# Attention and gated MLP on one core: weight conversions given written places, loads placed further ahead, and a memory turn done by transpositions

## The chip, the cores and the metric

The kernel runs on one core of one Trainium2 chip. The time is device microseconds (us) of one execution; times of a kernel are the median of several runs. The core has a matrix engine (TensorE, here PE), a vector engine (VectorE, DVE), a scalar engine (ScalarE, ACT), a GpSimd engine (POOL) and a sync engine (SP) whose instruction queue issues nearly all DMA transfers. Each engine works through its own instructions in order and waits for the others through semaphores.

## The reference

Two stages. A causal attention over 4 batches, 8 heads, 576 positions and 64 dimensions is mixed with a recall from a memory matrix, and the result goes through a gated MLP of 2304 tokens (512 to 1536 to 512).

```python
local = softmax(scale * q @ k.T, causal) @ v
q_p   = where(q > 0, q, exp(q) - 1) + 1
mem   = (q_p @ M_prev) / (q_p @ z_prev + 1e-6)
g     = sigmoid(beta)
x     = g * mem + (1 - g) * local          # then [B*S, H*D] = 2304 x 512
out   = (silu(x @ w_gate) * (x @ w_val)) @ w_out
```

All inputs arrive wide: the weights are read as pairs of 32-bit words and converted on the chip into a high and a low part that TensorE takes one after the other.

## The kernel before

**Attention.** The 32 heads are done as 16 pairs (`Pair`). One turn of the loop over `n` computes the scores and exponentials of pair `n` and finishes pair `n-1` (`old`): it turns its weighted probabilities by transpositions on PE (`turned1`, `turned`; the records tr<-ident,ps, tr<-ident,pl and tr<-ident,p), recalls from the memory (`recall`; tr<-mm,ph), turns the recalled 128x128 blocks (`recalled`; tr<-ident,mem) into two PSUM banks called `first` and `rest`, and adds the probabilities times V on top of them (`values`; tr<-g,vp). ACT and DVE then read `first` and `rest` out (`leave`; xh, xl). Turned blocks are copied out of PSUM as `g` by ACT or DVE. PSUM has four banks for scores (`psS`, records s) and four for everything else (`psT`, records tr), given out in rotation by `rot`; a bank is written again only when its last reader is through.

**Order.** Instructions called through `pe`, `act`, `dve` and `pool` stay in the order of the program text. Instructions called through `ACT`, `DVE` and `SP` may be placed by a scheduler, which works from a simulated timeline; `later_by` lowers their priority. The engines then run the resulting order strictly.

**Weights.** The MLP's weights come as 36 "thirds" (12 blocks of the hidden dimension, three matrices each). For a third n, `raw_load(n)` transfers it (wraw, 512 KB), `raw_top(n)` makes `we` from it on ACT, and `third(n)` makes `wa` from both on DVE in three instructions (min/max, shift, or) and copies the high part on ACT (wgh, woh); `low_part` later makes the low part on DVE (wgl, wol). wdr and wdo are DRAM copies for later token blocks. Thirds 0 to 2 are converted during the attention, at loop turns 1 to 3 (`EARLY`), through the scheduler. Thirds 3 and 4 are loaded when the attention ends; the others follow, one per PE step, while the first token block of the MLP runs (`some`).

**MLP.** Three blocks of 768 tokens (`ORDER`), for each of which all 12 hidden blocks are gone through: `eight` in the first token block (steps of 12 matmuls s<-xp..,wg., alternating between two PSUM banks, `bank`), `seven` in the others, with the second product (woh, wol) in between. In `eight`, a step with gv=0 is read by ACT (Silu, zg and zh), one with gv=1 by DVE.

Of the kernel before, what the change touches and what calls it, by code (L numbers as in the profile page):

```python
# [9 lines left out]
F32 = mybir.dt.float32  # L10
F32R = mybir.dt.float32r
I32 = mybir.dt.int32
AF = mybir.ActivationFunctionType
ALU = mybir.AluOpType
# [12 lines left out]

P_LOAD = 400
ORDER = (0, 768, 1536)
EARLY = (1, 2, 3)  # L30
P_EARLY = 200
ACT_K = (0, 1)
ON_POOL = ("q", "k")
PS_S, PS_T = 4, 4
# [4 lines left out]
W_TOP = float.fromhex("0x1.dffffep+15")  # L39
# [4 lines left out]
def attention_moe(ctx: ExitStack, tc: tile.TileContext, qt, kt_, v, m, beta, wg, wv, wo, out):  # L44
    nc = tc.nc
    PE, ACT, DVE, POOL, SP = nc.tensor, nc.scalar, nc.vector, nc.gpsimd, nc.sync
# [3 lines left out]
    psT = ctx.enter_context(tc.tile_pool(name="psT", bufs=1, space=PSUM))  # L50
# [43 lines left out]
    def rot(pool, name, shape, dtype, n):  # L94
        held = slots.setdefault(name, [0, []])
        if len(held[1]) < n:
            held[1].append(pool.tile(shape, dtype, name=f"{name}{len(held[1])}"))
        held[0] += 1
        return held[1][(held[0] - 1) % n]
# [6 lines left out]
        return pool.tensor_scalar(dst, src, 1.0, 0.0, op0=ALU.mult, op1=ALU.add)  # L106

    def split_lo(dst, src, hi, kind=""):
        eng = pool if kind in ON_POOL else DVE
        return eng.tensor_tensor(dst, src, hi.bitcast(F32), op=ALU.subtract)  # L110

    ident = const.tile([128, 128], F32, name="ident")
# [42 lines left out]

    held, wout = {}, {}
    thirds = [(f, j) for f in range(NF) for j in range(3)]
    raws, tops, low_parts = {}, {}, []

    def raw_load(n, after=None):  # L160
        if n < len(thirds):
            f, j = thirds[n]
            raws[n] = rot(wp, "wraw", [128, 512, 2], I32, 2)
            ld = SP.dma_start(raws[n].rearrange("p a b -> p (a b)"), (wg, wv, wo)[j][f].bitcast(I32))
            if after is not None:
                follow(ld, after, "the loads that the attention waits for go first")

    def raw_top(act, n):
        if n < len(thirds):
            tops[n] = rot(wp, "we", [128, 512], F32, 2)  # L170
            act.activation(tops[n], raws[n][:, :, 1].bitcast(F32), AF.Prelu, scale=2.0**-111, alpha=2.0**32)

    def low_part(dve):
        while low_parts:
            f, j, a, oh, ol = low_parts.pop()
            dve.tensor_tensor(ol, a, oh.bitcast(F32), op=ALU.subtract)
            if j == 2:
                for i, o in enumerate((oh, ol)):
                    SP.dma_start(wdo[f, :, i], o.bitcast(F32))

    def third(act, dve, n):

        low_part(dve)
        if n >= len(thirds):
            return
        f, j = thirds[n]
        e, low = tops.pop(n), raws.pop(n)[:, :, 0]
        dve.tensor_scalar(e, e, W_TOP * 2.0**-111, -W_TOP * 2.0**-79, op0=ALU.min, op1=ALU.max)
        a = rot(wp, "wa", [128, 512], I32, 3)
        dve.tensor_scalar(a, e.bitcast(I32), 3, None, op0=ALU.logical_shift_left)  # L190
        dve.scalar_tensor_tensor(
            out=a, in0=low, scalar=29, in1=a, op0=ALU.logical_shift_right, op1=ALU.bitwise_or
        )
        if j == 0:
            held[f] = [rot(wp, f"wg{part}", [128, 1024], F32R, 2) for part in "hl"]
        if j == 2:
            wout[f] = oh, ol = [rot(wp, f"wo{part}", [128, 512], F32R, 3) for part in "hl"]
        else:
            c = slice(j * 512, j * 512 + 512)
            oh, ol = (x[:, c] for x in held[f])  # L200
            SP.dma_start(wdr[f, :, c], a.bitcast(F32))
        act.copy(oh, a.bitcast(F32))
        low_parts.append((f, j, a.bitcast(F32), oh, ol))

    with tc.tile_pool(name="sb", bufs=1, reuse_waits="tile") as sb:

# [17 lines left out]
        def pair_split(n, raw):  # L224
            qr, kr = raw
            q = [rot(sb, f"q{part}", [128, 640], F32R, NK) for part in "hl"]
            k = [rot(sb, f"k{part}", [128, 576], F32R, NK) for part in "hl"]
            early = n == 0
            (ACT.copy if n in ACT_K else split_hi)(k[0], kr)
            split_hi(q[0], qr[:, 128:768])  # L230

            def lows():
                split_lo(q[1], qr[:, 128:768], q[0], "" if early else "q")
                split_lo(k[1], kr, k[0], "" if early else "k")

            return q, k, lows

# [20 lines left out]
        class Pair:  # L258
# [128 lines left out]

            def recalled(self):

                rest, first = (rot(psT, "tr", [128, 512], F32, PS_T) for _ in range(2))  # L390
                self.av = first, rest
                y = self.mem.rearrange("p t j d -> p t (j d)")
                for t in (2, 3, 0, 1):
                    o = t % 2 * 128
                    pe.matmul(self.av[t // 2][:, o : o + 128], y[:, t], ident, start=(t % 2 == 0), stop=False, skip_group_check=True)

            def turned(self, t, h, *engs):

# [72 lines left out]
        pairs[0].load()  # L471
        gates()
        pairs[0].split()
        pairs[0].load_v()
        pairs[0].phi_parts()()
        pairs[1].load()
        pairs[0].lows()
        nothing = lambda *args: None
        ending = lambda: nothing
        for n in range(NP + 1):  # L480
            cur = pairs[n] if n < NP else None
            old = pairs[n - 1] if n > 0 else None
            after = pairs[n + 1] if n + 1 < NP else None
            exp = cur.exp if cur else nothing
            scores = cur.scores if cur else lambda t: nothing
            turned, turned1 = (old.turned, old.turned1) if old else (nothing, nothing)
            if cur:
                cur.begin()
            if old:
# [12 lines left out]
            turned1(1, act)  # L502
            exp(0, 1)
            exp(1, 0)
            turned(2, 0, dve)
            turned(2, 1, dve)
            exp(1, 1)
            scale = old.recall() if old else nothing
            if cur:
                cur.weighed(((0, 0), (0, 1), (1, 0), (1, 1)))  # L510
            scale()
            if after:
                after.lows()
            phi = after.phi_parts() if after else nothing
            reads = [scores(t) for t in range(2, 4)]
            reads[0](0)
            reads[0](1)
            exp(2, 0)
            exp(2, 1)
            turned(3, 0, act)  # L520
            turned(3, 1, dve)
            read4 = cur.scores4() if cur else nothing
            reads[1](0)
            turned(4, 0, act, dve)
# [12 lines left out]
            ending = old.leave() if old else lambda: nothing  # L537
            if n + 2 < NP:
                with later_by(P_LOAD):
                    pairs[n + 2].load()  # L540
            if after:
                after.load_v()
            if n in EARLY:
                with later_by(P_EARLY):
                    i = EARLY.index(n)
                    raw_load(i, loads[n + 1])
                    raw_top(ACT, i)
                    third(ACT, DVE, i)
                    low_part(DVE)

        ending()()

# [1 line left out]
    with tc.tile_pool(name="stg2", bufs=1, reuse_waits="tile") as stg2, \  # L554
# [209 lines left out]
        first = units[0][0]  # L764
        for p, i, j in (("p1", 0, 0), ("p2", 0, 1), ("p7", 1, 0), ("p4", 1, 1)):
            direct(first, p, i, j)
        raw_load(3)
        raw_load(4)
        before = None
        spreads = lambda mix, *what: [  # L770
            (high if kind == "h" else low)(mix, p, k) for kind, p in what for k in range(2)
# [2 lines left out]
        for n, unit in enumerate(units):  # L774
# [5 lines left out]
            again(n)  # L780
            if whole and left:
                def some(i):
                    if i == 3:
                        raw_top(act, 3)
                    third(act, dve, i)
                    raw_top(act, i + 1)
                    raw_load(i + 2)
                for k in range(3):
                    plan[k].append(lambda i=3 * n + 3 + k: some(i))
            if n < len(units) - 1 and units[n + 1][0] != first:  # L790
# [106 lines left out]
```

## Time and profile before

| | |
|---|---|
| median of 3 runs | 651.28 us (648.32 to 651.58) |
| the profiled execution | 653.73 us |
| its span, first to last instruction | 651.8 us |
| mean granted TensorE clock | 0.988 of full speed |
| attention, up to the first MLP matmul | 212.1 us |
| PE busy | 627.0 us, 96% of the span |
| DVE, ACT, POOL busy | 460.0, 362.7, 156.0 us |

The time of the profiled execution is 1.9 us longer than its span, which is what lies before the first and behind the last instruction. A PE record's duration is modelled and overlaps the next record; what a matmul takes out of PE's time is read from the distance of two starts.

### The profile page before, as it was taken

How to read it: one execution, taken by the hardware profiler on the slowest of the kernel's cores; microseconds unless marked ns; L12 is line 12 of the kernel's file. 1: busy time of each engine (PE TensorE's matmuls, PEld its weight loads, DVE VectorE, ACT ScalarE, POOL GpSimd, SP SyncE). 2: the span in 40 equal slices, each digit the busy share in tenths (PEclk: the TensorE clock that was granted, in tenths of full speed). 3: DMA queues.
4: the chain of work that ended last, by engine and by line, in shares of the span. 5: the costliest groups of instructions: out<-in, count | busy, mean ns of one | idle time of the engine just before them, and what ended most of it. 6: DMA issues, size and time to landing. Idle time of an engine off the chain costs nothing.

```text
span 651.8 us, 11300 instructions
## 1 busy us (share of the span) xinstructions
PE 627.0 (96%) x3912; PEld 558.4 (86%) x3912; DVE 460.0 (71%) x1151; ACT 362.7 (56%) x838; POOL 156.0 (24%) x217
## 2 busy tenths in 40 slices
PE   3889999999999899999999999999999999999997
PEld 2767878878787799999999999999999999999995
DVE  4878887878876567667686666665688756666653
ACT  6667887878874444434445565454445744445342
POOL 4667878878783000000000000000000000000000
PEclk9979999999999899999999999999999999999999
DMA  7466557554331676688765561222646533232102
GB/s 216 133 207 203 167 159 219 158 146 153 100 110 42 220 237 198 208 283 284 255 211 171 201 209 66 98 97 76 214 163 223 182 117 109 66 113 81 65 32 98
DMA packets 48744, 102.46 MB, mean 157 GB/s; under 512 B 6960, under 2 KB 16176, under 8 KB 48688
## 3 DMA queue, kind: packets, MB, share of 16 engines
q1 hardware_dynamic: 48544, 101.45, 48.0%
q8 instruction: 31, 0.51, 0.4%
q10 hardware_dynamic: 144, 0.29, 0.1%
q14 instruction: 25, 0.20, 0.1%
HBM read 74.99 MB, written 26.74 MB: 156 GB/s over the span
## 4 chain that ended last, share of the span: by engine, by line
PE 84%; DVE 5%; ACT 4%; DMA 4%; issue 2%; POOL 1%; DVEq 0%; SPq 0%; ACTq 0%; POOLq 0%
PE s L83 52%; PE tr L83 32%; ACT pl L83 3%; DMA wraw<-in_wo_dram 2%; ACT g L83 1%; DVE mem L83 1%; DMA wraw<-in_wg_dram 1%; DVE pl L83 1%; DVE w L83 1%; DMA qr<-in_qt_dram 1%; DVE rs L83 1%; POOL ps L83 0%; DMA out_dram<-pt 0%; POOL ql L83 0%; POOL kl L83 0%
## 5 line engine op out<-in xcount | busy, mean ns | idle before, releaser
L83 PE MATMUL tr<-woh,uh 128*128 128x512 f32 x144 | 57.3, 398 | 0.0
L83 PE MATMUL tr<-wol,uh 128*128 128x512 f32 x144 | 56.7, 394 | 0.0
L83 PE MATMUL tr<-woh,ul 128*128 128x512 f32 x144 | 56.5, 393 | 0.0
L83 POOL TENSOR_SCALAR pl<-pl,rs,og 128x384 f32<-128x384 f32 (+1 forms) x64 | 44.8, 715 | 29.8 <-DVE rs L83 23.8
L83 ACT ACTIVATE pl<-pl,mx 128x384 f32<-128x384 f32 (+1 forms) x64 | 42.4, 665 | 15.0 <-DVE mx L83 15.0
L83 ACT ACTIVATE zh<-zh 128x384 f32<-128x384 f32 x24 | 12.7, 530 | 67.8 <-DVE zh L83 67.8
L83 PE MATMUL tr<-g,vp 128*64 128x320 f32 (+4 forms) x448 | 48.7, 360 | 0.0
L83 PE MATMUL s<-kh,qh 64*128 64x128 f32 (+4 forms) x160 | 37.2, 389 | 11.2 <-ACT gs L142 6.9
L83 DVE TENSOR_TENSOR zv<-s,zv 128x384 f32<-128x384 f32 x24 | 13.4, 558 | 47.1 <-PE s L83 47.1
L83 PEld LDWEIGHTS tr<-g,vp 128*64 128x64 f32 x448 | 29.4, 137 | 16.9
L83 DVE CUSTOM_DVE_ANT_0 pl<-s,maskp 128x384 f32<-128x384 f32 (+1 forms) x64 | 38.1, 616 | 0.0
L83 POOL TENSOR_SCALAR ps<-ps,rs,og 128x128 f32<-128x128 f32 (+1 forms) x64 | 32.3, 518 | 14.4 <-DVE rs L83 14.0
L83 DVE COPY g<-tr 128x384 f32<-128x384 f32 (+1 forms) x64 | 32.1, 522 | 3.0 <-PE tr L83 1.8
L83 ACT ACTIVATE ps<-ps,mx 128x128 f32<-128x128 f32 (+1 forms) x64 | 28.8, 457 | 9.5 <-DVE mx L83 9.5
L83 ACT COPY g<-tr 128x384 f32<-128x384 f32 (+1 forms) x64 | 31.5, 529 | 4.3 <-DVE w L83 2.2
L83 PEld LDWEIGHTS tr<-ident,pl 128*128 128x128 f32 x224 | 24.7, 144 | 9.9 <-issue 7.3
L83 PEld LDWEIGHTS s<-kh,qh 64*128 64x128 f32 (+1 forms) x160 | 19.3, 198 | 16.2 <-issue 7.1
L83 PEld LDWEIGHTS tr<-woh,ul 128*128 128x128 f32 x144 | 27.1, 188 | 7.0 <-DVE ul L83 0.3
L83 DVE TENSOR_TENSOR tl<-tt,th 128x512 fp32r<-128x512 f32 x48 | 32.8, 684 | 0.0
L83 ACT CAST th<-tt 128x512 fp32r<-128x512 f32 x48 | 30.0, 624 | 4.8 <-DVE tt L83 2.0
L83 PE MATMUL tr<-ident,pl 128*128 128x128 f32 x224 | 32.0, 285 | 0.6 <-DVE xl L83 0.6
L83 PE MATMUL s<-kl,qh 64*128 64x128 f32 (+4 forms) x160 | 31.9, 334 | 0.7 <-DVE kl L110 0.6
(187 smaller groups left out, 1960.6 us busy)
## 6 DMA issues: line engine op xcount, KB each, us to landing
wr<-wdr SPq DMA_DIRECT2D x24, 512.0 KB, 3.3
qr<-in_qt_dram SPq DMA_DIRECT2D x16, 384.0 KB, 3.3
wraw<-in_wg_dram SPq DMA_DIRECT2D x12, 512.0 KB, 4.1
wdr<-wa SPq DMA_DIRECT2D x24, 256.0 KB, 2.7
wraw<-in_wv_dram SPq DMA_DIRECT2D x12, 512.0 KB, 3.9
wraw<-in_wo_dram SPq DMA_DIRECT2D x12, 512.0 KB, 4.5
wol<-wdo SPq DMA_DIRECT2D x24, 256.0 KB, 2.8
woh<-wdo SPq DMA_DIRECT2D x24, 256.0 KB, 3.2
```

What stands on the lines that cost most here:

```text
L83: ins = getattr(eng, name)(*args, **kw)
```

## The change

There are five edits.

1. `recalled` marks its four 128x128 products with the identity as transpositions (`is_transpose=True`), and takes its two PSUM banks in the other order: `first` gets the bank that `rest` had. V is added on top as before. The two 64-wide products of `values` stay as they were.
2. Thirds 0 to 2 are no longer converted at loop turns 1 to 3 through the scheduler but at turns 2 to 11, in written places through `act` and `dve`: with `EARLY` = (2, 5, 8), a third is loaded one turn ahead, gets its `raw_top` at turn `at`, its first two DVE instructions (`third_bits`) a turn later, the rest (`third_word`) another turn later and its low part in the turn after that. All of them stand at the end of a turn, behind the read-out of `first`.
3. Thirds 3, 4 and 5 are loaded at turns 11, 12 and 13 (`AHEAD`), and third 3 gets its `raw_top` at turn 13. The loads of thirds 3 and 4 behind the attention are gone; `some(i)` loads third i+3 instead of i+2.
4. There are three wraw buffers instead of two.
5. For pair 0, k's high part is an in-order ACT copy ahead of the exponentials of phi, its low parts (k first, then q) come before phi, and pair 1's low parts on POOL come before the weighting of pair 0's first probabilities.

```diff
-EARLY = (1, 2, 3)
-P_EARLY = 200
+EARLY, AHEAD = (2, 5, 8), (11, 12, 13)
...
-            raws[n] = rot(wp, "wraw", [128, 512, 2], I32, 2)
+            raws[n] = rot(wp, "wraw", [128, 512, 2], I32, 3)
...
+    def third_bits(dve, n):
+        e = tops[n]
+        dve.tensor_scalar(e, e, W_TOP * 2.0**-111, -W_TOP * 2.0**-79, op0=ALU.min, op1=ALU.max)
+        wa[n] = a = rot(wp, "wa", [128, 512], I32, 3)
+        dve.tensor_scalar(a, e.bitcast(I32), 3, None, op0=ALU.logical_shift_left)
+
+    def third_word(act, dve, n):
         f, j = thirds[n]
...
+        tops.pop(n)
+        a, low = wa.pop(n), raws.pop(n)[:, :, 0]
         dve.scalar_tensor_tensor(
             out=a, in0=low, scalar=29, in1=a, op0=ALU.logical_shift_right, op1=ALU.bitwise_or
         )
...
-                rest, first = (rot(psT, "tr", [128, 512], F32, PS_T) for _ in range(2))
+                first, rest = (rot(psT, "tr", [128, 512], F32, PS_T) for _ in range(2))
...
-                    pe.matmul(self.av[t // 2][:, o : o + 128], y[:, t], ident, start=(t % 2 == 0), stop=False, skip_group_check=True)
+                    pe.matmul(
+                        self.av[t // 2][:, o : o + 128], y[:, t], ident, start=(t % 2 == 0), stop=False, is_transpose=True,
+                        skip_group_check=True,
+                    )
...
-            if n in EARLY:
-                with later_by(P_EARLY):
-                    i = EARLY.index(n)
-                    raw_load(i, loads[n + 1])
-                    raw_top(ACT, i)
-                    third(ACT, DVE, i)
-                    low_part(DVE)
+            for i, at in enumerate(EARLY):
+                if n == at - 1:
+                    raw_load(i, loads[n + 2])
+                if n == at:
+                    raw_top(act, i)
+                if n == at + 1:
+                    third_bits(dve, i)
+                if n == at + 2:
+                    third_word(act, dve, i)
+                if n == at + 3:
+                    low_part(dve)
+            if n in AHEAD:
+                raw_load(len(EARLY) + AHEAD.index(n), loads[n + 2])
+                if n == AHEAD[-1]:
+                    raw_top(act, len(EARLY))
...
-        raw_load(3)
-        raw_load(4)
...
                 def some(i):
-                    if i == 3:
-                        raw_top(act, 3)
                     third(act, dve, i)
                     raw_top(act, i + 1)
-                    raw_load(i + 2)
+                    raw_load(i + 3)
```

On PE the sequence of instructions stays the same in kind and number. This is what stands in one turn of the attention at the turn of the recalled blocks, before (tr_284 and tr_289 are two PSUM banks; what an instruction waits for stands in brackets):

```order
L83 MATMUL tr_272<-ident,p_215 128x128 [waits Pool_49]
L83 MATMUL tr_272<-ident,p_215 128x128 x3
L83 MATMUL tr_277<-ident,p_215 128x128
L83 MATMUL tr_284<-ident,mem_295 128x128 [waits Activation_49]
L83 MATMUL tr_284<-ident,mem_295 128x128
L83 MATMUL tr_289<-ident,mem_295 128x128 [waits DVE_49]
L83 MATMUL tr_289<-ident,mem_295 128x128
L83 MATMUL tr_289<-g_247,vp_132 64x256 [waits DMAHW4_49]
```

And in the changed kernel:

```order
L82 MATMUL tr_272<-ident,p_215 128x128 [waits Pool_49]
L82 MATMUL tr_272<-ident,p_215 128x128 x3
L82 MATMUL tr_277<-ident,p_215 128x128
L82 MATMUL tr_289<-ident,mem_295 128x128 [waits DVE_49]
L82 MATMUL tr_289<-ident,mem_295 128x128
L82 MATMUL tr_284<-ident,mem_295 128x128 [waits Activation_49]
L82 MATMUL tr_284<-ident,mem_295 128x128
L82 MATMUL tr_284<-g_247,vp_134 64x256 [waits DMAHW6_49]
```

The bank that DVE empties is now taken first and the one that ACT empties second, and the V products start in the latter.

On DVE, this is what stood in pair 0's part before, from the reading of its fourth score tile on (ISA pl and ISA p read scores, mx is the maximum that goes with each):

```order
L83 ISA pl_223,mx_149<-s_159,maskp 128x512
L83 ISA mx_149 128x1
L188 TENSOR_SCALAR we_408<-we_408 128x512
L83 ISA pl_225,mx_149<-s_160,maskp 128x512
L83 ISA mx_149 128x1
L190 TENSOR_SCALAR wa_411<-we_408 128x512
L83 ISA p_215,mx_149<-s_151,maskp 128x288
L83 ISA mx_149 128x1
L191 SCALAR_TENSOR_TENSOR wa_411<-wraw_406,wa_411 128x512
L83 ISA p_215,mx_149<-s_152,mask_89,mx_149 128x288
```

In the changed kernel the same place reads:

```order
L82 ISA pl_223,mx_149<-s_159,maskp 128x512
L82 ISA mx_149 128x1
L82 ISA pl_225,mx_149<-s_160,maskp 128x512
L82 ISA mx_149 128x1
L82 ISA p_215,mx_149<-s_151,maskp 128x288
L82 ISA mx_149 128x1
L82 ISA p_215,mx_149<-s_152,mask_89,mx_149 128x288
```

Third 0's instructions have left this place; they now stand behind the read-out of `first` of pairs 2 to 4.

On ACT, this is the beginning of the MLP before (zg and zh are the Silu of the steps 0 and 2 of the first hidden block, we the `raw_top` of thirds 3, 4 and 5):

```order
L83 ACT_TABLE_LOAD
L83 ACTIVATE zg_2524<-s_152 128x384
L83 ACTIVATE we_566<-wraw_564 128x512
L83 CAST wgh_2530<-wa_411 128x512
L83 ACTIVATE we_408<-wraw_406 128x512
L83 CAST uh_2549<-zg_2524 128x384
L83 CAST wgh_2530<-wa_569 128x512
L83 ACTIVATE we_566<-wraw_564 128x512
L83 ACTIVATE zh_2573<-s_152 128x384
```

And in the changed kernel:

```order
L82 ACT_TABLE_LOAD
L82 ACTIVATE zg_2527<-s_152 128x384
L82 CAST wgh_2532<-wa_701 128x512
L82 ACTIVATE we_553<-wraw_849 128x512
L82 CAST uh_2551<-zg_2527 128x384
L82 CAST wgh_2532<-wa_1137 128x512
L82 ACTIVATE we_993<-wraw_1285 128x512
L82 ACTIVATE zh_2575<-s_152 128x384
```

One `we` is gone from here, and the last `we` ahead of zh reads a third wraw buffer, whose load was issued in the attention.

## Rows read from the trace of the kernel before

**Rows 1.** The page, part 2: PE's busy tenths in 40 equal slices of the span.

```profile
PE   3889999999999899999999999999999999999997
```

**Rows 2.** Timeline of PE, one turn: start, length, what, count.

```profile
105.66 1.16 PE L83 MATMUL tr<-ident,mem 128*128 128x128 f32 x8
106.75 0.87 PE L83 MATMUL tr<-g,vp 128*64 128x256 f32 x8
...
109.72 0.33 PE L83 MATMUL s<-kh,qh 64*128 64x128 f32 x2
...
111.48 0.85 PE L83 MATMUL tr<-ident,pl 128*128 128x128 f32 x6
...
114.80 1.09 PE L83 MATMUL tr<-ident,pl 128*128 128x128 f32 x8
115.64 0.38 PE L83 MATMUL s<-kh,qh 128*128 128x288 f32 x1
...
116.53 0.71 PE L83 MATMUL tr<-ident,p 128*128 128x128 f32 x5
117.32 1.16 PE L83 MATMUL tr<-ident,mem 128*128 128x128 f32 x8
```

**Rows 3.** The chain that ended last, same turn: start, length, what.

```profile
111.48 1.98 PE tr L83 x16
...
116.80 0.48 ACT g L83
```

**Rows 4.** Timeline of PE: the memory turns of pairs 0, 2 and 14.

```profile
29.65 1.16 PE L83 MATMUL tr<-ident,mem 128*128 128x128 f32 x8
...
59.03 1.16 PE L83 MATMUL tr<-ident,mem 128*128 128x128 f32 x8
...
199.10 1.16 PE L83 MATMUL tr<-ident,mem 128*128 128x128 f32 x8
```

**Rows 5.** Timeline of DVE, start of the kernel; idle before it in brackets.

```profile
12.92 0.69 DVE L83 CUSTOM_DVE_ANT_0 pl<-s,maskp 128x512 f32<-128x512 f32 x1
...
15.36 0.62 DVE L188 TENSOR_SCALAR we<-we 128x512 f32<-128x512 f32 x1 [1.75 <-ACT we L171]
...
18.42 0.51 DVE L83 CUSTOM_DVE_ANT_0 p<-s,mask,mx 128x288 f32<-128x288 f32 x1
```

**Rows 6.** Timelines of ACT and PE, third 2 in the attention.

```profile
38.37 0.68 ACT L171 ACTIVATE we<-wraw 128x512 f32<-128x512 f32 x1 [2.90 <-DMA wraw<-in_wo_dram]
...
39.47 2.54 PE L83 MATMUL tr<-mm,ph 128*128 128x130 f32 x10 [2.92 <-ACT g L83]
```

**Rows 7.** Timelines of ACT and PE, the beginning of the MLP.

```profile
220.15 0.62 ACT L83 CAST wgh<-wa 128x512 fp32r<-128x512 f32 x1 [1.31 <-DVE wa L83]
222.68 0.66 ACT L83 ACTIVATE we<-wraw 128x512 f32<-128x512 f32 x1 [1.91 <-DMA wraw<-in_wo_dram]
223.24 0.47 ACT L83 ACTIVATE zh<-s 128x384 f32<-128x384 f32 x1
...
223.77 0.69 PE L83 MATMUL s<-xp1h,wgh 128*128 128x384 f32 x1 [3.05 <-ACT zh L83]
```

**Rows 8.** Windows: busy us of PE, PEld, DVE, ACT, POOL; PE's granted clock; DMA.

```profile
223.70:229.40 5.70, 5.63 (x18) 5.63 (x19) 4.30 (x9) 2.14 (x6) 0.00 (x0) 0.50 0.79 256
...
39.40:44.90 5.50, 5.43 (x24) 4.45 (x25) 4.60 (x15) 4.11 (x12) 1.60 (x5) 0.50 0.21 44
110.60:112.20 1.60, 1.60 (x15) 1.38 (x14) 1.58 (x10) 1.44 (x5) 1.60 (x3) 1.00 0.73 144
```

**Rows 9.** Timeline of DVE, the same turn as rows 2.

```profile
104.28 0.69 DVE L83 COPY g<-tr 128x512 f32<-128x512 f32 x1
...
110.42 0.29 DVE L83 CUSTOM_DVE_ANT_0 ps<-s,maskp 128x128 f32<-128x128 f32 x1 [1.26 <-POOL pl L83]
...
110.85 0.49 DVE L83 TENSOR_TENSOR xl<-tr,xh 128x320 fp32r<-128x320 f32 x1
```

**Rows 10.** Groups by line: a third's last DVE step; busy us, mean ns, idle.

```profile
L83 DVE SCALAR_TENSOR_TENSOR wa<-wraw,wa 128x512 int32<-128x512 int32 x33 | 22.9, 693 | 1.1
```

More of the change, by code (lines that the diff above doesn't have):

```diff
@@ L108, in split_lo @@
     def split_lo(dst, src, hi, kind=""):
-        eng = pool if kind in ON_POOL else DVE
+        eng = pool if kind in ON_POOL else dve
         return eng.tensor_tensor(dst, src, hi.bitcast(F32), op=ALU.subtract)
@@ L157, in attention_moe @@
     thirds = [(f, j) for f in range(NF) for j in range(3)]
-    raws, tops, low_parts = {}, {}, []
+    raws, tops, wa, low_parts = {}, {}, {}, []
     def raw_load(n, after=None):
@@ L179, in low_part @@
                     SP.dma_start(wdo[f, :, i], o.bitcast(F32))
[L181 to L185, printed above, removed]
+    def third_bits(dve, n):
[4 more added lines that the diff above has]
+    def third_word(act, dve, n):
         f, j = thirds[n]
[L187 to L190, printed above, removed]
+        tops.pop(n)
+        a, low = wa.pop(n), raws.pop(n)[:, :, 0]
         dve.scalar_tensor_tensor(
@@ L203, in third @@
         low_parts.append((f, j, a.bitcast(F32), oh, ol))
+    def third(act, dve, n):
+        low_part(dve)
+        if n < len(thirds):
+            third_bits(dve, n)
+            third_word(act, dve, n)
     with tc.tile_pool(name="sb", bufs=1, reuse_waits="tile") as sb:
@@ L228, in pair_split @@
             early = n == 0
-            (ACT.copy if n in ACT_K else split_hi)(k[0], kr)
+            (act.copy if early else ACT.copy if n in ACT_K else split_hi)(k[0], kr)
             split_hi(q[0], qr[:, 128:768])
             def lows():
+                if early:
+                    split_lo(k[1], kr, k[0])
                 split_lo(q[1], qr[:, 128:768], q[0], "" if early else "q")
-                split_lo(k[1], kr, k[0], "" if early else "k")
+                if not early:
+                    split_lo(k[1], kr, k[0], "k")
             return q, k, lows
@@ L473, in attention_moe @@
         pairs[0].split()
+        pairs[0].lows()
         pairs[0].load_v()
@@ L476, in attention_moe @@
         pairs[1].load()
-        pairs[0].lows()
         nothing = lambda *args: None
@@ L508, in attention_moe @@
             scale = old.recall() if old else nothing
+            if n == 0:
+                after.lows()
             if cur:
@@ L511, in attention_moe @@
             scale()
-            if after:
+            if after and n:
                 after.lows()
@@ L542, in attention_moe @@
                 after.load_v()
-            if n in EARLY:
-                with later_by(P_EARLY):
-                    i = EARLY.index(n)
-                    raw_load(i, loads[n + 1])
-                    raw_top(ACT, i)
-                    third(ACT, DVE, i)
-                    low_part(DVE)
+            for i, at in enumerate(EARLY):
[8 more added lines that the diff above has]
+                if n == at + 3:
+                    low_part(dve)
+            if n in AHEAD:
+                raw_load(len(EARLY) + AHEAD.index(n), loads[n + 2])
+                if n == AHEAD[-1]:
+                    raw_top(act, len(EARLY))
         ending()()
```

## The prediction

> **What bounds the kernel now.** I read the page first, then PE's timeline turn by turn, then the chain that ended last, then the places where PE's row has a bracket. PE is busy throughout; only the first slices and the slice around 220 us stay below 9 tenths [rows 1]. Those lengths are modelled, so the start-to-start distances decide.
>
> In a regular turn of the attention the memory's turn starts at 105.66 and again at 117.32: 11.66 us per pair [rows 2], and from pair 2 at 59.03 to pair 14 at 199.10 it is twelve times 11.67 [rows 4]. The chain says what makes up these 11.66: PE until 111.48 + 1.98 = 113.46, then 3.8 us of DVE and ACT work that ends with ACT's copy of turned probabilities at 116.80 + 0.48 = 117.28, and the next memory turn follows 0.04 later [rows 3]. So two thirds of a turn are PE's own work, and the last third is a chain of other engines that releases a PSUM bank. PE works in that third too, and waits at its end.
>
> Three places are irregular. In pair 0, DVE stands still for 1.75 us because third 0's first instruction sits between two score readings and its data is late [rows 5]. At 38.37 ACT waits 2.90 us for third 2's load, the copies behind it are late, and PE idles 2.92 us [rows 6]. At the beginning of the MLP ACT waits 1.91 us for third 5's load with the Silu `zh` behind it, and PE idles 3.05 us [rows 7]. Behind the last two idles the granted clock is 0.50, for 5.5 and 5.7 us [rows 8]. After that the MLP has no gap [rows 1], so whatever is won before 230 us should arrive at the end in full.
>
> **The change, part by part.**
>
> *Products to transpositions.* The eight records of the four products run from 105.66 to 106.75, 0.136 us each, two records per product. Eight transpositions of the same shape run from 114.80 to 115.64, 0.105 us each, one record per transposition [rows 2]. Four of them cost 0.42 instead of 1.09: 0.67 us per pair off PE. The Trainium skill, "TensorE: Matmul & The Clock Gate", Part 4, puts a 128x128 transposition at about 275 ns in a kernel; by that four cost 1.10 and this edit would save nothing. The distances in this trace are less than half of it, and I go by them.
>
> *The other bank first.* The five transpositions of p start at 116.53 and would be through 0.53 later, at 117.06; the product starts at 117.32 because its bank is the one that ACT's copy releases at 117.28: 0.26 us of waiting [rows 2, 3]. In the new order the first two transpositions use the bank that DVE's copy releases, 104.28 + 0.69 = 104.97 one turn earlier [rows 9], well before 105.40. They take 0.21, and ACT's bank is wanted at 105.61 and free at 105.66. The V products then start at 105.87 instead of 106.75: 0.88 in all, 0.21 of it from the wait. The six transpositions at 111.48 start right behind xl, which ends at 110.85 + 0.49 = 111.34 [rows 2, 9]; three of them now use the bank that is read out earlier. That is worth between nothing and three transpositions (0.3); I take 0.1, since the other three still need xl. Together 0.98 per turn.
>
> *Thirds 0 to 2 in the turns.* In nine turns DVE gets one more piece behind the reading-out of `first`: 0.69 us [rows 10], or two instructions that I estimate at 0.85 together from the same row (lighter operations of the same width). DVE idles there for 1.26 now [rows 9]. The shorter turn takes up to 0.98 of that, so 0.28 is left and 0.4 to 0.6 of each piece may show in nine of fourteen turns unless another slack takes it. ACT's pieces stand where ACT waits for `rest`. Costs between 0 and 0.4 per turn; I take 0.15. A turn then saves 0.98 - 0.15 = 0.83 and lasts 10.8. Fourteen turns (pair 0 to pair 14) give 11.6 us; bounds 0.45 and 1.1 per turn, 6.3 and 15.4. Pairs 14 and 15 save their own products once more at the end, 1.3 us.
>
> *The start.* Without third 0 the score readings of pair 0 follow one another. The one at 12.92 ends at 13.61; two more of at most 0.69 each and the last of 0.51 end by 15.5, where they now end at 18.93 [rows 5]. That is 3.4 at least, and the chain behind it (exponential, weighting, transpositions) is unchanged. Third 1's DVE work also leaves pair 0's path, and the first low parts come ahead of phi; together 0 to 1.5. I take 4.4, bounds 3 and 5.
>
> *Third 2's wait.* From pair 0's turn to pair 2's it is 29.38 us [rows 4] where two regular turns are 23.3: 6.0 lost, which fits 2.92 of idling plus half of 5.5 us at half clock. Third 2 is now loaded a full turn before ACT asks for it, and at a place where ACT would wait anyway. All 6.0 come back; bounds 5 and 6.1.
>
> *The beginning of the MLP.* Now 3.05 of idling plus half of 5.7 at half clock: 5.9 at most. With third 5 there in time, `we` follows the copy that ends at 220.77, then `zh`: 0.66 and 0.47 more, 221.9 instead of 223.71 [rows 7]. That alone leaves 1.2 us of idling. But third 3's DVE work no longer waits for a `we` behind the first Silu, so DVE's row of conversions starts earlier by about one 0.69 piece and its waits; I expect 0.3 of idling to be left, too short to cost the clock. Gain 5.2; bounds 1.9 (1.2 of idling and the clock falls all the same) and 5.9.
>
> *Loads.* Every wraw load goes ahead of a vp load in SP's queue, and both are used about a turn later; I cost that at nothing. If this cover failed, PE would stall as it does for third 2, about 5.7 per case. The third buffer has no cost in time.
>
> **Sum.** 4.4 + 6.0 + 11.6 + 1.3 + 5.2 = 28.5 us. The profiled execution took 653.73, so 625.2; the median of the runs is 2.45 below it, so 622.8. I predict 623 us.
>
> **The rivals.**
>
> *A, ACT's copy stays the gate.* The new order wants ACT's bank 0.05 us before it is free, so any delay of ACT shows in full: with a copy 0.5 late a turn saves 0.3 to 0.4. For it: the chain already ends there [rows 3], and ACT gets three more pieces per third. Against: their place. Time 629 to 630. The skill's 275 ns would lead near the same place, since only the waits would be saved.
>
> *B, a regular turn isn't shortened at all,* because DVE and ACT need their 11.66 anyway and PE idles instead. Against: DVE has a 1.26 us hole in the turn. Then only start, third 2, end and MLP count: 16.9, time 634.
>
> *C, a wait comes back,* at the MLP's first steps (1.9 instead of 5.2) or as one load that ACT waits for in the attention (5.7). Time 626 to 629.
>
> *D, slower: the clock falls in the attention.* Nine transpositions would now follow one another where five preceded products. If TensorE fell to 1.2 GHz there, PE's share of a turn, 113.46 - 105.66 = 7.8 us, would become up to 15.6, as in the stretch at 39.40 [rows 8]. From four such turns on the gain of 28.5 is gone; in all fifteen it would be some 730 us. Against: the stretch from 110.60 holds twelve transpositions with nothing between them but bank changes, at a granted clock of 1.00 [rows 8]. The same Part 4 of the skill's TensorE page says that the full clock does not engage for transpositions, which speaks for D; that window speaks against it.
>
> **How the numbers follow.** My forecast (618 to 628) 0.68; A 0.12; B 0.06; C 0.08; D 0.03; no change, because something unseen binds, 0.03. Lowest saving by the bounds: 3 + 5 + 6.3 + 0.9 + 1.9 = 17.1, 634; highest 5 + 6.1 + 15.4 + 1.4 + 5.9 = 33.8, 617.5. With B taken in, the range is 616 to 636. Half a per cent, 3.3 us, is about what a measurement here can tell from no change. Faster 0.93, the same 0.03, slower 0.04.
>
> **What the changed profile would show.** Sixty-four records of tr<-ident,mem 128x128 where there were 128, 0.105 apart; the distance from one memory turn to the next near 10.8, with turns that carry a DVE piece a little longer; pair 0's turn near 25 and pair 2's near 47; no idle bracket above 1 us on PE after the first 20 us; granted clock 1.00 from there on, the half-clock stretches gone. The prediction is wrong if the turn stays above 11.2 (A, B), if ACT's `we` or PE show a bracket that ends on wraw (C), or if a clock below 1.00 shows in the regular turns (D).

## The result and the profile after

The changed kernel takes **630.79 us** (median of 4 runs, 630.26 to 631.08); the kernel before, measured beside it, 651.43 (4 runs, 648.32 to 655.12). The ratio is 0.968, 95% interval 0.963 to 0.973: 20.6 us less. The forecast was 623, its range 616 to 636. The profiled execution of the changed kernel took 630.26 us with a span of 628.4, at a mean granted clock of 0.999; the one before had a span of 651.8, so the two traces differ by 23.4 us.

The page after, part 2 (busy tenths in 40 slices), PE and POOL:

```profile
PE   4999999999999999999999999999999999999997
POOL 5898998988960000000000000000000000000000
```

PE's row has lost its 8s, behind the first slice and in the fourteenth [rows 1]. POOL's row, of which the prediction says nothing, is mostly 8 and 9 through the attention and 0 behind it; as a share of the whole span that is only 25%.

Timeline of PE after: the memory turns of pairs 0 and 2, one turn that carries no piece of a third, and the memory turn of pair 14:

```profile
24.86 0.72 PE L82 MATMUL tr<-ident,mem 128*128 128x128 f32 x4
...
46.77 0.72 PE L82 MATMUL tr<-ident,mem 128*128 128x128 f32 x4
...
159.95 0.73 PE L82 MATMUL tr<-ident,mem 128*128 128x128 f32 x4
160.61 0.87 PE L82 MATMUL tr<-g,vp 128*64 128x256 f32 x8
...
165.17 0.95 PE L82 MATMUL tr<-ident,pl 128*128 128x128 f32 x6
...
170.34 0.71 PE L82 MATMUL tr<-ident,p 128*128 128x128 f32 x5
170.88 0.72 PE L82 MATMUL tr<-ident,mem 128*128 128x128 f32 x4
...
181.82 0.73 PE L82 MATMUL tr<-ident,mem 128*128 128x128 f32 x4
```

Four records where [rows 2] have eight. From one memory turn to the next it is now 170.88 - 159.95 = 10.93 us, where it was 11.66. The memory turn follows the five transpositions of p by 0.54, where it was 0.79: the wait in front of it is gone. Pair 0's turn stands at 24.86 (29.65 in [rows 4]), pair 2's 21.91 later (29.38), pair 14's 135.05 after pair 2's (140.07).

Timelines of ACT and PE at the beginning of the MLP, and windows over the stretch behind it and over the one where third 2 was late:

```profile
201.90 0.67 ACT L82 ACTIVATE we<-wraw 128x512 f32<-128x512 f32 x1
202.47 0.47 ACT L82 ACTIVATE zh<-s 128x384 f32<-128x384 f32 x1
...
202.99 0.44 PE L82 MATMUL s<-xp1h,wgh 128*128 128x384 f32 x1 [0.28 <-ACT zh L82]
```

```profile
203.00:208.70 5.70, 5.70 (x31) 5.43 (x32) 4.38 (x10) 2.06 (x5) 0.00 (x0) 1.00 0.92 287
39.00:44.50 5.50, 5.50 (x58) 4.73 (x55) 4.55 (x21) 4.96 (x15) 5.05 (x8) 1.00 0.77 240
```

PE waits 0.28 us where [rows 7] show 3.05, `we` no longer waits for its load, and the clock is 1.00 in both places where [rows 8] show 0.50.

**Where the 23.4 us of the two traces come from**, by start-to-start distances:

| | predicted | measured |
|---|---|---|
| start, to pair 0's memory turn | 4.4 | 4.8 |
| third 2's wait (pair 0 to 2, beyond two turns) | 6.0 | 6.0 |
| fourteen turns, pieces of thirds included | 11.6 | 6.5 |
| pairs 14 and 15 to the first MLP matmul | 1.3 | 0.7 |
| the MLP (439.7 to 434.3) | 5.2 | 5.4 |
| sum | 28.5 | 23.4 |

One term is off: the turns. A turn without a piece takes 10.93 where 10.68 was worked out, and the nine turns with pieces take 3.9 us more together where 2.1 was allowed (one by one they scatter, from 10.83 to 12.01 by PE's memory turns). The experiments ask what holds a turn at 10.93.

The trace gave the theory that they test. Timeline of POOL after, one turn without a piece (the same as above):

```profile
153.28 2.81 POOL L82 TENSOR_SCALAR pl<-pl,rs,og 128x384 f32<-128x384 f32 x4 [1.17 <-ACT xh L82]
156.06 0.83 POOL L82 TENSOR_SCALAR p<-p,rs,og 128x576 f32<-128x576 f32 x1
156.85 0.68 POOL L82 TENSOR_SCALAR kh<-kr 128x576 fp32r<-128x576 f32 x1
157.50 0.73 POOL L82 TENSOR_SCALAR qh<-qr 128x640 fp32r<-128x640 f32 x1
158.21 1.95 POOL L82 TENSOR_SCALAR ps<-ps,rs,og 128x128 f32<-128x128 f32 x4
160.13 1.56 POOL L82 TENSOR_TENSOR ql<-qr,qh 128x640 fp32r<-128x640 f32 x1
161.64 1.41 POOL L82 TENSOR_TENSOR kl<-kr,kh 128x576 fp32r<-128x576 f32 x1
```

and of DVE, where that 1.17 us comes from:

```profile
161.90 1.83 DVE L82 SCALAR_TENSOR_TENSOR ph<-qe,ph 128x640 f32<-128x640 f32 x1
163.65 0.16 DVE L82 TENSOR_SCALAR rs<-sm 128x5 f32<-128x5 f32 x1
163.85 0.19 DVE L82 RECIPROCAL rs<-rs 128x5 f32<-128x5 f32 x1
```

POOL works 9.76 us without a pause and stands only between `kl` and the next weighting `pl` (164.21), which needs `rs`. In front of `rs` DVE has `ph`, which took 0.89 us before the change and takes 1.83 here: it starts 0.26 behind the start of POOL's `kl` and ends 0.68 after its end. That end is the same before the change and after it, and also in most turns with a piece, where `ph` starts later and its record is 1.20 long: `kl`'s end sets it, and a longer record is not by itself a loss. The bracket names ACT's xh; but by the names `pl` reads `rs`, and in other turns with the same 1.17 the bracket names DVE's rs. The Trainium skill, "SBUF — State Buffer", section "SBUF: two separate sides", says that DVE and GpSimd share one pair of SBUF ports as an exclusive lock: a DVE operation with two SBUF inputs, or in a two-port mode, and a GpSimd operation exclude each other for the whole instruction. The 1.83, which ends behind `kl`, agrees.

### The profile page after: what moved, and what is told of

Its sections match the earlier page's. It is cut to its first block, busy times and chain, and to the rows that moved or that the text cites. A ratio compares the mean times of both kernels' runs of the same rounds, so it can differ in the third digit from the quotient of the medians.

```text
span 628.4 us, 11188 instructions
## 1 busy us (share of the span) xinstructions
PE 612.1 (97%) x3848; PEld 544.2 (87%) x3848; DVE 464.2 (74%) x1151; ACT 359.2 (57%) x838; POOL 159.0 (25%) x217
## 4 chain that ended last, share of the span: by engine, by line
PE 90%; DVE 5%; ACT 2%; issue 1%; DMA 1%; SPq 0%; POOLq 0%; DVEq 0%; POOL 0%
PE s L82 58%; PE tr L82 31%; DMA kr<-in_kt_dram 1%; DVE pl L82 1%; DVE ph L82 1%; DVE p L82 1%; DVE xl L82 1%; ACT ps L82 1%; DVE rs L82 0%; DVE wa L82 0%; ACT pl L82 0%; ACT wgh L82 0%; DVE mem L82 0%; DVE g L82 0%; ACT g L82 0%
## 5 line engine op out<-in xcount | busy, mean ns | idle before, releaser
L82 POOL TENSOR_SCALAR pl<-pl,rs,og 128x384 f32<-128x384 f32 (+1 forms) x64 | 49.2, 782 | 23.3 <-DVE rs L82 14.8
L82 DVE SCALAR_TENSOR_TENSOR zg<-s,zg 128x384 f32<-128x384 f32 x36 | 20.0, 557 | 20.3 <-PE s L82 19.5
L82 DVE TENSOR_TENSOR zg<-s,zp 128x384 f32<-128x384 f32 x24 | 13.4, 557 | 25.1 <-ACT bh L82 19.8
```

What stands on the lines that cost most here:

```text
L82: ins = getattr(eng, name)(*args, **kw)
```

## The experiments

Theory **L**: DVE's instructions that read and write SBUF stand until POOL's instruction beside them ends, and the loop of the two (POOL's 9.76 us and the waits for `rs`) sets the turn. Theory **P**: PE's own work sets it, as the prediction had it. Theory **A**: the bank that ACT's copy releases does (rival A). Every kernel was timed against the kernel before on the same chip; medians here, and turns from their traces. Kernels 1 to 4, 5 to 8 and 9 to 12 ran on three chips, on which the kernel before took 649.97, 650.67 and 651.96, so that a difference of one or two us between medians of different groups says little; the turns and the ratios do.

| kernel | median us | ratio to before (95%) | turn without piece | POOL's waits in it |
|---|---|---|---|---|
| before | 651.43 | | 11.66 | 0.42 + 1.45 |
| changed | 630.79 | 0.968 (0.963, 0.973) | 10.93 | 1.17 |
| 1 transpositions alone | 643.06 | 0.990 (0.987, 0.993) | 11.61 | 0.41 + 1.41 |
| 2 bank order alone | 645.92 | 0.993 (0.990, 0.996) | 11.62 | 0.41 + 1.40 |
| 3 edit 1 alone | 636.47 | 0.981 (0.976, 0.986) | 10.94 | 1.17 |
| 4 changed, edit 1 undone | 641.85 | 0.987 (0.984, 0.990) | 11.65 | 0.45 + 1.42 |
| 5 as 1, no add | 638.49 | 0.981 (0.977, 0.984) | 11.06 | 1.29 |
| 6 changed, no add | 625.83 | 0.963 (0.960, 0.965) | 10.66 | 0.89 |
| 7 changed, ph late | 640.12 | 0.984 (0.982, 0.987) | 11.32 | 1.14 |
| 8 changed, kh on ACT | 630.29 | 0.969 (0.967, 0.972) | 10.97 | 0.41 + 1.42 |
| 9 changed, pieces spread | 631.46 | 0.970 (0.967, 0.973) | 10.91 | 1.17 |
| 10 as 9, no add | 625.67 | 0.961 (0.958, 0.964) | 10.67 | 0.89 |
| 11 changed, raw_top(3) late | 631.60 | 0.970 (0.966, 0.973) | 10.96 | |
| 12 changed, edit 5 undone | 632.93 | 0.972 (0.969, 0.975) | 10.98 | |

**1 to 4: edit 1 in parts.** In the kernel before, once one of these two edits, once both; and the changed kernel without them.

```diff
-                rest, first = (rot(psT, "tr", [128, 512], F32, PS_T) for _ in range(2))
+                first, rest = (rot(psT, "tr", [128, 512], F32, PS_T) for _ in range(2))
...
-                    pe.matmul(self.av[t // 2][:, o : o + 128], y[:, t], ident, start=(t % 2 == 0), stop=False, skip_group_check=True)
+                    pe.matmul(
+                        self.av[t // 2][:, o : o + 128], y[:, t], ident, start=(t % 2 == 0), stop=False, is_transpose=True,
+                        skip_group_check=True,
+                    )
```

Transpositions alone:

> The kernel before with is_transpose on the four products alone, banks in the old order. Four records instead of eight save 0.67 us behind the bank's release: L and P alike 11.66 - 0.67 = 10.99 per turn, still above the floor of 10.93: 14 x 0.67 + 0.7 to 1.3 = 10 to 10.7 off, 641. A: the next turn's ACT copy does not come earlier with it, so the product waits longer for its bank and little is left: 648 or more.

The bank order alone:

> The kernel before with the other bank order alone, the products kept. P: 0.26 of waiting goes, 0.2 to 0.3 per turn, turn 11.4, 3 to 4.3 off: 647 to 648. L: the same, as 11.4 is above the floor of 10.93. A: nothing, since ACT's bank is then wanted 0.5 later than it is free only if ACT is not late: 651.

Both:

> The kernel before with edit 1 alone (transpositions and the other bank order). Theory L, the loop of POOL and DVE: in the changed kernel's turns without a piece of a third, POOL works without a pause from its weighting pl to kl (9.76 us), and then idles 1.17 us, always the same, while DVE's ph waits for kl's end and rs follows it; 10.93 us is a floor that PE's saving cannot go below. A turn then falls from 11.66 to 10.93: 14 x 0.73 + 0.7 at the end = 10.9 us off, 640.5. Theory P, PE alone, as in the prediction: 14 x 0.98 + 1.3 = 15 off, 636. Theory A, ACT's copy stays the gate of the bank: turn 11.3, about 646.

The changed kernel without both:

> The changed kernel with edit 1 undone (products, banks in the old order), all else kept. L: with turns of 11.66 POOL and DVE have about 0.7 us to spare, which takes the pieces of thirds 0 to 2; they cost near nothing and edit 1 was worth only 14 x 0.46 + 0.7 = 7: 637 to 638. If the pieces cost what they cost in the changed kernel whatever the turn (3.9 us over nine turns, against the free turn), edit 1 was worth 10.9: 641 to 642. P: 638.7 by the prediction's 0.98 per turn, with pieces of 0.15.

Each half alone takes 0.04 to 0.05 us off a turn, both together 0.72. No theory had expected that. A fits the turn of each half, but not that of both; P fits none; L had the floor of both together (10.94 for 10.93) and was wrong on each half. The times of 1 and 2 lie lower than 0.05 per turn would give, because in their traces the MLP also takes 435.2 and 435.6 us instead of 439.7 (PE waits 1.55 and 1.65 at its beginning instead of 3.05); the turns are the test. In kernel 3 the MLP takes 435.6, and third 2 makes ACT wait for no load, so that pairs 0 to 2 are 24.88 apart instead of 29.38: its 636.47 is P's number by chance, and its turns are L's. Why these two waits shrank there was not tried.

What holds the halves at 11.6 stands in the trace of kernel 1 (transpositions alone). POOL, and DVE beside it:

```profile
124.05 0.73 POOL L83 TENSOR_SCALAR qh<-qr 128x640 fp32r<-128x640 f32 x1
125.19 0.45 POOL L83 TENSOR_SCALAR ps<-ps,rs,og 128x128 f32<-128x128 f32 x1 [0.41 <-ACT ph L83]
```

```profile
124.22 0.58 DVE L83 TENSOR_SCALAR rs<-sm 128x4 f32<-128x4 f32 x1
124.84 0.18 DVE L83 RECIPROCAL rs<-rs 128x4 f32<-128x4 f32 x1
```

`rs<-sm` handles four columns. It starts 0.17 behind the start of POOL's `qh` and ends with it, 0.58 later; in kernel 2 it takes 0.65 and ends with `qh` too; in the kernel before it comes just as `qh` ends and takes 0.11. In all three `ps` follows 0.41 to 0.42 behind `qh`, whatever PE has saved. With both halves (kernel 3) `rs` comes 0.12 *ahead of* `kh`, the POOL instruction in front of `qh`:

```profile
138.34 0.17 DVE L83 TENSOR_SCALAR rs<-sm 128x4 f32<-128x4 f32 x1
```

```profile
138.46 0.68 POOL L83 TENSOR_SCALAR kh<-kr 128x576 fp32r<-128x576 f32 x1
```

Then `ps` needs no wait and the whole 0.42 goes at once, and with it 0.3 of the other wait. In six of the changed kernel's nine turns with a piece `rs` starts while `kh` runs; it stands until `kh` ends and still comes ahead of `qh`, and `ps` doesn't wait. So the gain of edit 1 is a threshold: DVE gets its tiny instruction in ahead of `qh`, or it is done only when `qh` ends. One of these six, DVE and POOL:

```profile
100.53 0.34 DVE L82 TENSOR_SCALAR rs<-sm 128x4 f32<-128x4 f32 x1
```

```profile
100.18 0.66 POOL L82 TENSOR_SCALAR kh<-kr 128x576 fp32r<-128x576 f32 x1
100.82 0.72 POOL L82 TENSOR_SCALAR qh<-qr 128x640 fp32r<-128x640 f32 x1
101.53 1.94 POOL L82 TENSOR_SCALAR ps<-ps,rs,og 128x128 f32<-128x128 f32 x4
```

Kernel 4 came out at 641.85 with 11.65 in turns without a piece and 12.02 to 12.15 in the nine with one: pieces cost 0.4 to 0.5 there also, although POOL and DVE had more idle time. L's "they cost near nothing" was wrong.

**5: the same tiny instruction taken away.** The kernel before with transpositions alone, without the add in front of the reciprocal. The edit removes both `rs<-sm` of a turn, that of four columns and that of five.

```diff
-                dve.tensor_scalar(rs, self.sm[:, c : c + n], 1.0e-9, None, op0=ALU.add)
-                dve.reciprocal(rs, rs)
+                dve.reciprocal(rs, self.sm[:, c : c + n])
```

> The kernel before with the transpositions alone, and without the DVE instruction rs<-sm that adds 1e-9 to sums which are 1 or more (the reciprocal reads sm itself; the values are the same in fp32). Theory L (DVE's instructions that read and write SBUF stand until POOL's instruction beside them ends): with the transpositions alone, rs<-sm starts 0.18 behind POOL's qh and takes 0.57 us instead of 0.11 to 0.17, until qh ends, in every regular turn; the memory, the score readings, ACT's exponentials and the bank that PE waits for follow it, and so the turn stayed at 11.61. Without it the turn falls to about 11.1, 12 x 0.5 = 6 us: 637. Rival A (ACT's copy is the gate by its own work): rs is not what it waits for, turn 11.6, 643. If the reciprocal is held in the same way: 11.6 too, but then it shows 0.5 us or more in the trace.

```profile
127.22 2.80 POOL L83 TENSOR_SCALAR pl<-pl,rs,og 128x384 f32<-128x384 f32 x4 [1.29 <-DVE rs L83]
```

The turn is 11.06 and POOL's wait at `ps` is gone (its waits are the 1.29 at `pl`): L's number, and A falls, since ACT's copies are the same. The time, 638.49, is 1.5 above the 637 given.

**6: the same edit in the changed kernel.**

> The changed kernel without rs<-sm, as above. L: rs<-sm and the gap behind it are 0.20 us of the 1.17 in which POOL stands between kl and the weighting pl, turn 10.93 to 10.73, 14 x 0.2 = 2.8 off: 628. P (PE's own work sets the turn): 630.8, unchanged.

625.83, and 10.66 per turn, 0.07 better than L gave. POOL waits 0.89 instead of 1.17; `ph` ends 0.68 behind `kl` as before, 0.20 goes with `rs<-sm` and the gap behind it, and `pl` follows the reciprocal by 0.10 instead of 0.17, which nothing here explains:

```profile
160.59 2.81 POOL L82 TENSOR_SCALAR pl<-pl,rs,og 128x384 f32<-128x384 f32 x4 [0.89 <-PE tr L82]
```

9.76 + 0.89 is 10.65, and PE's timeline shows no wait in this turn any more: memory turn to V products 0.53 (0.66 in the changed kernel), the second block of tr<-ident,pl 0.82 long (0.95).

```profile
156.93 0.60 PE L82 MATMUL tr<-ident,mem 128*128 128x128 f32 x4
157.46 0.87 PE L82 MATMUL tr<-g,vp 128*64 128x256 f32 x8
...
162.03 0.82 PE L82 MATMUL tr<-ident,pl 128*128 128x128 f32 x6
...
167.59 0.60 PE L82 MATMUL tr<-ident,mem 128*128 128x128 f32 x4
```

PE's own work is therefore no more than 10.66, what the prediction had worked out as 10.68, and the changed kernel loses 0.27 per turn to the loop.

**7: ph behind rs.**

```diff
-            phi()
             if cur:
                 cur.weighed(((2, 0), (2, 1), (3, 0), (3, 1), (4, 0)))
+            phi()
```

> The changed kernel with DVE's ph behind rs instead of ahead of it. L: POOL's weighting no longer waits for a ph that stands until kl ends; rs then follows ACT's sum, which is there 0.1 before kl ends, so POOL stands 0.3 to 0.4 instead of 1.17; ph then runs beside POOL's weighting, which may grow by 0.4 as it does beside the pieces. Turn 10.93 to about 10.5, 14 x 0.4 = 6 off: 625; at worst, with the weighting longer by as much as POOL won, 631. P: unchanged, 631. If xl, now behind the same DVE work, comes late for PE's transpositions: slower, 633 or more.

Slower than the changed kernel by 9.3 us. Only the last case has the sign, and not for its reason. Timelines of DVE and POOL:

```profile
161.15 0.17 DVE L82 TENSOR_SCALAR rs<-sm 128x5 f32<-128x5 f32 x1 [0.99 <-ACT p L82]
161.35 0.19 DVE L82 RECIPROCAL rs<-rs 128x5 f32<-128x5 f32 x1
161.46 0.79 DVE L82 SCALAR_TENSOR_TENSOR ph<-qe,ph 128x640 f32<-128x640 f32 x1
```

```profile
161.72 3.20 POOL L82 TENSOR_SCALAR pl<-pl,rs,og 128x384 f32<-128x384 f32 x4 [1.14 <-DVE rs L82]
```

`ph` had covered DVE's wait for ACT's last sum; now DVE stands 0.99 for it and runs `ph` afterwards, so POOL's wait is as long as before (1.14), and `ph` lengthens POOL's weighting from 2.80 to 3.20. 9.76 + 0.40 + 1.14 = 11.3, the measured turn. The cost on POOL was expected, the gain was not there. That is some 5.5 of the 9.3 us; most of the rest lies in six of the nine turns with a piece, which take 12.3 to 12.45: there `rs` is held by `qh` again.

**8: less work on POOL.** The high part kh by ACT in all pairs.

```diff
-            (act.copy if early else ACT.copy if n in ACT_K else split_hi)(k[0], kr)
+            act.copy(k[0], kr)
```

> The changed kernel with the high part kh copied by ACT, in program order, instead of POOL, in all pairs. POOL has 0.65 us less per turn, ACT 0.62 more. L: turn 10.93 to about 10.5, where PE's own work with its small waits stands: 6 off, 625. A: ACT's work is in the chain that frees the bank, turn up to 11.5, 639. P: 631.

630.29: nothing, and L fails here. Rows of POOL, and DVE's `rs`:

```profile
153.53 2.80 POOL L82 TENSOR_SCALAR pl<-pl,rs,og 128x384 f32<-128x384 f32 x4 [1.17 <-DVE rs L82]
...
157.10 0.73 POOL L82 TENSOR_SCALAR qh<-qr 128x640 fp32r<-128x640 f32 x1
158.24 1.95 POOL L82 TENSOR_SCALAR ps<-ps,rs,og 128x128 f32<-128x128 f32 x4 [0.41 <-DVE rs L82]
...
164.51 0.66 POOL L82 TENSOR_SCALAR pl<-pl,rs,og 128x384 f32<-128x384 f32 x1 [1.42 <-DVE rs L82]
```

```profile
157.51 0.35 DVE L82 TENSOR_SCALAR rs<-sm 128x4 f32<-128x4 f32 x1
```

POOL's 0.65 turned into waits: `qh` has moved up to where `kh` was, `rs` stands behind it again (0.35), and `ps` waits 0.41. So POOL's work alone isn't the bound; what counts is when DVE's instructions meet POOL's. That the turn ends at the same 10.97 is a coincidence, as far as the traces show it; no run tests it (this kernel without the add would).

Cut at the end of `qh`, the turns without a piece of all kernels so far that keep the add fall into the same two parts. From the start of `pl` to the end of `qh` is POOL's own run: 4.95 us, 4.30 without `kh` (kernel 8), 5.34 with `ph` beside `pl` (kernel 7); beside the pieces of the changed kernel it is 5.4 to 5.5. From the end of `qh` to the next `pl` it takes 6.0 where `rs` got in ahead of `qh` (kernels 3, 7 and the changed one), and 6.7 where it did not (before, 1, 2, 4 and 8). Kernel 8 has the shorter first part and the longer second, 4.30 + 6.68; the changed kernel has 4.95 + 5.99.

**9 and 10: pieces of thirds one by one.** One DVE instruction per turn in turns 3 to 14, the copy of the high part behind the exponentials of phi; the low parts come last.

```diff
+            if n - 4 in EARLY:
+                third_high(act, EARLY.index(n - 4))
+                late.append(low_parts.pop())
...
                 if n == at + 1:
                     third_bits(dve, i)
                 if n == at + 2:
-                    third_word(act, dve, i)
+                    third_shift(dve, i)
                 if n == at + 3:
-                    low_part(dve)
+                    third_word(dve, i)
+            if n >= EARLY[-1] + 4 and late:
+                low_parts.append(late.pop(0))
+                low_part(dve)
```

> The changed kernel with the pieces of thirds 0 to 2 spread: one DVE instruction per turn in turns 3 to 14 (min/max, shift, or, low) instead of two, one, one in nine turns, and ACT's copy of the high part behind the exponentials of phi, no longer ahead of the read-out of the bank that PE waits for. Pieces cost 3.9 us over the free turn in the changed kernel. Theory D (DVE's time behind xl, and ACT's copy that waits in line for DVE): single pieces of 0.43 to 0.69 find 0.3 of idle time each, and the copy is out of the way; 12 turns of 0.1 to 0.2 remain, 2 us: 629. Theory L as to POOL (a piece that reads and writes SBUF beside POOL's weighting lengthens it, 2.80 to 3.2 or 3.3): 12 turns of 0.43: 632. No difference if neither: 630.8.

> The same, without rs<-sm (which adds 1e-9 to sums that are 1 or more). There the free turn is PE's own 10.66 and the pieces cost 4.7 us. D: 2 to 2.5 remain, 623 to 624. L as to POOL: POOL has to spare now, 10.66 - 9.76 less the 0.6 that rs and the signal need, 0.3; 12 turns of 0.13 to 0.2, 623 as well. If the pieces cost their own length wherever they stand: 12 x 0.6 = 7, 628.

631.46, no better: D (the theory in the expectation, that the pieces lack room on DVE) falls, L has the sign and the size. POOL's weighting beside a min/max or shift, and beside an or, in kernel 9:

```profile
85.17 3.06 POOL L82 TENSOR_SCALAR pl<-pl,rs,og 128x384 f32<-128x384 f32 x4 [1.17 <-ACT xh L82]
...
107.58 3.33 POOL L82 TENSOR_SCALAR pl<-pl,rs,og 128x384 f32<-128x384 f32 x4 [1.16 <-ACT xh L82]
```

2.80 becomes 3.06 or 3.33, and nearly all turns with a piece are 11.2 or 11.46 to 11.49: 10.94 and that difference. The changed kernel has 3.23 and 3.33 in its nine turns, and from pl to pl 11.37 and 11.47. In kernel 10 the turns with a piece take 10.91 and 11.16, those without 10.66, and the time is 625.67, the same as kernel 6 (625.59 to 627.15 against 625.46 to 626.44). Both theories had given 623 or a little more for it; what POOL's weighting is lengthened by arrives in full, so at 10.66 the loop has nothing to spare either, just as PE.

**11: the hand-over.** raw_top(3) back in the first step of the MLP.

```diff
-                if n == AHEAD[-1]:
-                    raw_top(act, len(EARLY))
...
                 def some(i):
+                    if i == 3:
+                        raw_top(act, 3)
```

> The changed kernel with third 3's raw_top back in the first step of the MLP, ahead of the first Silu's successor. The prediction's account of the beginning of the MLP: we and then zh come 0.66 and 0.47 later, about 1.2 us of idling instead of 0.28, 0.9 more: 631.7; and if the granted clock falls behind it as it did before, 2.85 more: 634.6. If it is the load alone that mattered: 630.8.

631.60. PE waits 1.04 for `zh` instead of 0.28, and the clock stays at 1.00 behind it:

```profile
205.64 0.44 PE L82 MATMUL s<-xp1h,wgh 128*128 128x384 f32 x1 [1.04 <-ACT zh L82]
```

**12: edit 5 undone.** The old order of pair 0's splits, low parts and phi, and of pair 1's low parts; its core:

```diff
-        pairs[0].lows()
         pairs[0].load_v()
         pairs[0].phi_parts()()
         pairs[1].load()
+        pairs[0].lows()
```

> The changed kernel with edit 5 undone (order of pair 0's splits, low parts and phi, and of pair 1's low parts). The prediction gave the removal of third 0 from pair 0's readings 3.4 of the 4.4 us of the start, and edit 5 with third 1's DVE work 0 to 1.5; the start became 4.8 shorter, so edit 5 would be worth about 1.0: pair 0's turn near 25.9, 631.8. If edit 5 is the larger part, 27 or more: 633.

Pair 0's turn stands at 27.43, 2.6 later than in the changed kernel, and the median is 2.1 higher (1.5 above kernel 9, on the same chip). Kernels with the changed kernel's start differ among themselves (pair 0's turn at 24.3 to 26.0 in kernels 4, 6, 7, 9, 10 and 11), so edit 5 is worth 1.4 to 3.1 us, more than the 1.0 expected.

## Why the prediction was right, and where it was off

**Start (4.4, measured 4.8).** The sum was right by luck, its parts were not: with edit 5 undone, taking third 0 out of the readings is worth about 29.65 - 27.43 = 2.2, not 3.4, and edit 5 the other 2.6 (1.4 to 3.1, as starts differ), rather than 0 to 1.5. The readings did become 3.8 shorter in kernel 12 (their last one ends at 15.09, where it was 18.93), but the chain behind them was not unchanged, as the sum had it: `rs` stood until POOL's `kl` ended at 17.47.

```profile
15.49 1.98 POOL L82 TENSOR_TENSOR kl<-kr,kh 128x576 fp32r<-128x576 f32 x1
...
16.14 1.36 DVE L82 TENSOR_SCALAR rs<-sm 128x5 f32<-128x5 f32 x1
```

**Third 2's wait (6.0) and the beginning of the MLP (5.2).** Right as argued: idling and half clock both went, with the 0.3 of idling that was expected (0.28). Kernel 4 has both gains without edit 1 (pairs 0 to 2 are 23.31 apart, two of its turns, and the MLP takes 434.2), so they belong to edits 2 to 4; edit 1 alone happens to give a part of both as well (kernel 3). Kernel 11 shows by PE's wait (1.04 for 0.28) that the place of third 3's `we` is worth 0.8 of it.

**The fourteen turns (11.6, measured 6.5): the step that was mis-sized.** Two parts of it. First, 0.98 per turn was read from PE's rows. As a sum it was right for PE's own work: kernel 6 shows PE without a wait at 10.66. In its parts it was not: from the memory turn to the V products it is 0.53 where it was 1.09, which saves 0.56 and not 0.67; the wait of 0.25 went, and the transpositions of ps and pl take 0.20 less, where 0.21 and 0.1 were taken. And a turn was not PE's to set. The 11.66 before was POOL's 9.8 and two waits for DVE (0.42 and 1.45), and 10.93 is POOL's 9.76 and one wait of 1.17; PE has 0.27 left over, and it shows as 0.13 at ACT's bank and 0.13 at the second block of tr<-ident,pl. The prediction read the last third of a turn as a chain of DVE and ACT [rows 3] and left POOL out, whose 156 us are only a quarter of the span. Second, a piece was priced by DVE's idle time [rows 9], 2.1 us in all; it costs what POOL's weighting is lengthened by, 0.43 to 0.53 in each of nine turns, of which 3.9 us arrive in PE's distances. By the prediction's own sign, a turn above 11.2 for A or B, the outcome stands on the line: 10.93 without a piece, 11.36 on average with one, 11.21 over all fourteen.

**The end (1.3, measured 0.7).** The same: a turn saves 0.7, not 0.98.

**The transposition's price.** Right as a distance: consecutive records stand 0.11 us apart, and the five of p take 0.54; but four of them with the step to the V products take 0.53, not 0.42. The Trainium skill, "TensorE: Matmul & The Clock Gate", Part 4, has about 275 ns for one in a kernel and says that the full clock doesn't engage for them. A single record is 0.27 us long here as well, but the next one starts before it ends, so the 275 ns are not what each costs in a row. In a stretch where nine follow one another, from 114.20 on with other products before and behind them, the granted clock was 1.00:

```profile
114.10:115.70 1.60, 1.60 (x15) 1.23 (x16) 1.53 (x5) 1.60 (x5) 1.60 (x3) 1.00 1.02 384
```

**The rivals.** A gave 629 to 630 and nearly hit the time, by another mechanism: PE does wait for ACT's bank, but only for as long as DVE and POOL hold ACT up; in kernel 6 the same copy is no gate. B named the right kind of cause, other engines needing their turn, with the wrong engine and the wrong size. C and D didn't occur.

**The time.** 623 lay 7.8 below: 5.1 from the terms above, the rest because 2.45 was taken off for the profiled execution before, while the one after lies 0.5 below its median.

## What to carry to other kernels

A share of busy time over the whole span hides an engine that works in one stage only: look at each engine's row in the stage, and add up its work and its waits over one turn, for every engine, before calling one the bound. Where DVE and POOL work side by side on SBUF, place DVE's small instructions where POOL stands, or take them away: dropping the adds of four and five columns in front of a turn's reciprocals (which changes nothing for sums of 1 or more) was worth 4 to 5 us here (3.8 by the spans of the two traces, 5.0 by the medians), about a fifth of the whole change, and gives the fastest version (625.8 us). Two edits can be worth next to nothing each and 0.7 us per turn together, so neither is to be judged alone.

## What was not expected of the hardware

- An instruction on four columns (`rs<-sm`, 0.11 to 0.17 us) took 0.58 and 0.65 beside POOL's `qh`, and the one of five columns 1.36 beside `kl`; they ended with it. The reciprocal behind it, also from SBUF to SBUF, took 0.12 to 0.19 everywhere.
- `ph` (two SBUF inputs) took 0.79 where it started ahead of POOL's weighting, 0.89 before the change, where it started shortly ahead of the end of `kl`, and 1.83 where it started 0.26 behind the start of `kl`. Before and after the change it ended 0.68 behind the end of `kl` in the regular turns, wherever beside `kl` it had started.
- It works the other way round as well: POOL's weighting of 2.80 us took 3.06 to 3.33 with one or two DVE pieces beside it, and 3.20 with `ph` beside it.
